# Decode attention plus a token mixer: the values of two heads as one load of 64 KB rows

## The chip, the cores and the metric

The kernel runs on one core of a Trainium2 chip. The metric is the device time of one execution in microseconds. Before the change it is 1288.31 us, the median of 3 runs (1288.29 to 1288.52). The engines are named as in the profile: PE (matrix products), PEld (its weight loads), DVE (vector), ACT (scalar), POOL, and SP, which issues the loads.

## The reference

One decode step for 8 sequences: `x + attention(norm(x)) + mixer(norm(x))`, with 32 query heads, 8 key/value heads, 8192 cached positions and heads of 128, all in float32.

```
xn = layernorm(x)
q = (xn @ wq) -> (B, Hq, 1, Dh);  k, v = the caches, each kv head serves 4 query heads
p = softmax(q k^T * Dh**-0.5);    attn = (p v) -> (B, 1, Hq*Dh) @ wo
h = layernorm(xn);  y = (gelu(h * w1 + b1)) w2 + b2      # over the token axis, F = 1792
out = x + attn + y
```

The two caches are 256 MiB each, wq and wo 8 MiB each.

## The kernel before

The work is cut into 64 items, one for each sequence and kv head; `s` is the item. Item `s` uses the buffers `k = s % 2`. An item's keys and values are 4 MB each, loaded as 128 rows of 32 KB, row `p` holding 64 cached positions. K has two buffers in SBUF and V has two; wq first lies in the V buffers, and wo at the end in the K buffers.

For one item:

- `turn` (L238, DVE): four transposes in place of a quarter of K each, 32x32 blocks.
- `qk` (L244, PE): 16 products, in 4 column groups, all of which need all four quarters; the scores go to the PSUM bank `S[k]`.
- `sm_max`, `sm_bias`, `sm_exp` (L250 to L259): maximum per partition on DVE, a product on PE that spreads it, an addition and a minimum on DVE, the exponential on ACT with its sum per partition.
- `sm_place` and `sm_turn` (L263, L267): a product with a permutation on PE, and a transpose on DVE, which bring the weights into the form in which PE can hold them.
- `pv` (L274, PE): 16 products of the weights with V, into the bank `O[k]`.
- `o_pick`, `o_place`, `o_sums`, `o_norm` (L279 to L300): the blocks of `O` that count are masked, added up and divided by the sum of the weights; the result goes to the table `OX`.
- the mixer's share of the item (`mx_begin`, `mx_steps`, `mx_end`, `y_add`), on PE, ACT, POOL and DVE.

A function `slot` issues one such item in an order that is written out by hand, with the items overlapped: in slot `s` DVE turns K of item `s` and the weights of item `s - 1`, PE makes the scores of `s` and the value products of `s - 1`, and the output of `s - 2` is normed. The loop `For_i` has four slots, each a stage. A stage may not be entered by an engine before all engines have finished the stage before the last one; `previous_stage_wait` says where in its instructions an engine reports that.

All large loads are issued by SP in program order: V of item `s` at the head of slot `s`, once the value products of `s - 2` have left that buffer, and K of item `s + 2` after the score product of `s`. Ahead of the loop stand wq, K of items 0 and 1 and V of item 0; after it the last two slots issue wo in two halves (`load_wo`, L80), the second in ever smaller pieces. The end, after the last slot, is written out: the last value products (L274), the last norms, `regroup` (L438), which gathers the outputs of 7 of the 8 sequences within the last slot and of the eighth at the end, the product with wo (L471, L481), and the store of the result (L483).

Of the kernel before, what the change touches and what calls it, by code (L numbers as in the profile page):

```python
# [30 lines left out]
PAD = 96  # L31
# [3 lines left out]
def attn_mixer_kernel(ctx: ExitStack, tc: tile.TileContext, x, kc, vc, wq, wo, w1, b1, w2, b2, out):  # L35
# [11 lines left out]
    turns = [0]  # L47

    def misc():
        turns[0] += 1  # L50
        return MI[turns[0] % 2]

# [4 lines left out]
    V = [ring.tile([P, NT, DH], F32, name=f"v{k}") for k in range(2)]  # L57
    WQ = []

    def load_wq():  # L60
        for a in range(2):
            t = V[a].rearrange("p (c n) d -> p c (n d)", c=NC // 2)
            nc.sync.dma_start(t, wq.rearrange("(p c) n -> p c n", c=NC)[:, a * NC // 2:(a + 1) * NC // 2, :])
            WQ.extend(t[:, c, :] for c in range(NC // 2))

    def load(to, src, n, pieces=(NT,)):
        rows = src.rearrange("b h (p t) d -> (b h) p t d", p=P)[n]
        at = 0
        for w in pieces:
            nc.sync.dma_start(to[:, at:at + w, :], rows[:, at:at + w, :])  # L70
            at += w

# [3 lines left out]
    def load_wo(a, pieces):  # L76
        rows = wo.rearrange("(p a c) n -> a p c n", p=P, a=2)[a]
        at = 0
        for w in pieces:
# [34 lines left out]
                          ident.rearrange("p (g i x) -> p i g x", i=NB, g=NG))  # L114
    dm = const.tile([P, NG], F32, name="dm")
# [41 lines left out]
    RD = const.tile([P, REP], F32, name="rd")  # L157
# [44 lines left out]
    def q_project(between):  # L202
# [6 lines left out]
        for a in range(2):  # L209
            q = t2k.tile([P, n], F32, name="t2k")  # L210
            nc.scalar.copy(q, S[a])
            mt = O[a]
# [5 lines left out]
            mq = misc()  # L218
# [33 lines left out]
    def sm_bias():  # L252
        m = misc()
        nc.tensor.matmul(m[:, :P], MR.to_broadcast([P, P]), nident, start=True, stop=True)  # L254
        nc.vector.tensor_tensor(SQ, m[:, :P], hmask, ALU.add)  # L255
        nc.vector.tensor_reduce(NBIAS, SQ, AX.X, ALU.min)  # L256

    def sm_exp(k):
        nc.scalar.activation(PR[k], S[k], AF.Exp, bias=NBIAS, scale=SCALE, accum_out=LR[:, k:k + 1])  # L259

    def sm_place(k):
        m = misc()
        nc.tensor.matmul(m, perm, PR[k], start=True, stop=True)  # L263
        return m

    def sm_turn(k, m):
        nc.vector.transpose(PT[k], m)  # L267

    def pv(k, u0=0, u1=NU):
        for u in range(u0, u1):
            c = u % NB
            nc.tensor.matmul(O[k][c * Q:(c + 1) * Q, :], PT[k][:, u * Q:(u + 1) * Q],  # L274
                             V[k][:, u * NG:(u + 1) * NG, :].rearrange("p t d -> p (t d)"),
                             start=(u < NB), stop=(u >= NU - NB))

    def o_pick(k):
        nc.vector.tensor_tensor(OM.rearrange("p (g d) -> p g d", g=NG), O[k].rearrange("p (g d) -> p g d", g=NG),  # L279
# [4 lines left out]
    def o_place(k):  # L284
        nc.tensor.matmul(MH[:, k * REP:(k + 1) * REP], OB[:, :DH], sel, start=True, stop=True)  # L285

    def o_last(k):
        nc.vector.tensor_copy(OM[:, :256], O[k][:, :256])
        nc.scalar.copy(OM[:, 256:], O[k][:, 256:])
# [7 lines left out]
    def o_norm(k, s):  # L297
        nc.vector.reciprocal(RD, MH[:, 64 + k * REP:64 + (k + 1) * REP])  # L298
        nc.vector.tensor_tensor(OS, MH[:, k * REP:(k + 1) * REP], RD, ALU.mult)  # L299
        nc.vector.tensor_tensor(OX[:, s], OS.unsqueeze(2).to_broadcast([P, REP, NB]),  # L300
# [211 lines left out]
```

## Time and profile before

| | |
|---|---|
| median of 3 runs | 1288.31 us |
| the profiled execution's own time | 1288.28 us |
| its span | 1286.4 us |
| mean granted clock of PE | 0.818 |
| busy PE, DVE, ACT, POOL | 67%, 70%, 26%, 17% of the span |
| moved by DMA | 553.84 MB, mean 431 GB/s |

The span runs from the first to the last instruction of the profiled execution; its own time is 1.9 us longer. Busy shares are over the whole span: a PE or DVE that is busy two thirds of the time may still be waited for in every slot. In the timeline a row is a start, a length, an engine, a line of the kernel and what it writes and reads, and in brackets how long the engine had been idle and what ended that.

### The profile page before, as it was taken

How to read it: one execution, taken by the hardware profiler on the slowest of the kernel's cores; microseconds unless marked ns; L12 is line 12 of the kernel's file. 1: busy time of each engine (PE TensorE's matmuls, PEld its weight loads, DVE VectorE, ACT ScalarE, POOL GpSimd, SP SyncE). 2: the span in 40 equal slices, each digit the busy share in tenths (PEclk: the TensorE clock that was granted, in tenths of full speed). 3: DMA queues.
4: the chain of work that ended last, by engine and by line, in shares of the span. 5: the costliest groups of instructions: out<-in, count | busy, mean ns of one | idle time of the engine just before them, and what ended most of it. 6: DMA issues, size and time to landing. Idle time of an engine off the chain costs nothing.

```text
span 1286.4 us, 15585 instructions
## 1 busy us (share of the span) xinstructions
PE 863.0 (67%) x5498; PEld 256.8 (20%) x5498; DVE 895.1 (70%) x1261; ACT 332.6 (26%) x459; POOL 218.1 (17%) x201
## 2 busy tenths in 40 slices
PE   4568667667667667667667667667567667567578
PEld 1112112212212112112112112112112112112123
DVE  3687787677686676676686776686676776676672
ACT  1142232222222222232222222231231231231221
POOL 0121221121221221221221221221211221221210
PEclk9688788788778788788788788788788788788789
DMA  9999999999999999999999999999999999999998
GB/s 409 425 438 430 433 438 426 439 427 438 431 433 439 425 439 427 438 432 432 439 425 440 426 438 433 431 439 426 439 428 436 435 429 439 426 439 430 434 434 355
DMA packets 20206, 553.84 MB, mean 431 GB/s; under 512 B 2621, under 2 KB 2653, under 8 KB 3045
## 3 DMA queue, kind: packets, MB, share of 16 engines
q1 hardware_dynamic: 19764, 553.67, 99.8%
q8 instruction: 7, 0.11, 0.0%
q10 hardware_dynamic: 400, 0.02, 0.0%
q0 software_dynamic: 32, 0.02, 0.0%
q14 instruction: 3, 0.02, 0.0%
HBM read 553.69 MB, written 0.02 MB: 430 GB/s over the span
## 4 chain that ended last, share of the span: by engine, by line
DVE 50%; PE 34%; issue 9%; DMA 7%; DVEq 0%; ACT 0%; SPq 0%; ACTq 0%
DVE k L238 39%; PE s L244 28%; DMA k<-in_A_k_cache_dram 4%; DVE mr L250 3%; DVE pt L267 3%; PE misc L254 2%; DMA k<-in_A_wo_dram 2%; PE mh L285 2%; DVE sq L255 1%; PE o L274 1%; DVE nb L256 1%; DMA small<-in_B_w_dram 1%; DVE os L299 1%; DVE ox L300 1%; PE misc L263 1%
## 5 line engine op out<-in xcount | busy, mean ns | idle before, releaser
L238 DVE STREAM_TRANSPOSE k<-k 128x2048 f32<-128x2048 f32 x256 | 574.1, 2280 | 73.8 <-issue 52.6
L244 PE MATMUL s<-k,w 128*32 128x512 f32 x2048 | 368.5, 886 | 333.0 <-DVE k L238 324.6
L274 PE MATMUL o<-v,pt 128*32 128x512 f32 x2048 | 246.0, 598 | 0.0
L331 POOL TENSOR_TENSOR macc<-g,mw 112x512 f32<-112x512 f32 x64 | 66.5, 1040 | 976.7 <-ACT g L328 976.7
L244 PEld LDWEIGHTS s<-k,w 128*32 128x32 f32 x2048 | 86.7, 155 | 607.1 <-issue 404.2
L306 DVE TENSOR_TENSOR yacc<-mh,yacc 128x128 f32<-128x128 f32 x64 | 18.6, 291 | 228.6 <-PE mh L285 228.6
L259 ACT ACTIVATE pr<-s,nb 128x512 f32<-128x512 f32 x64 | 44.0, 688 | 493.6 <-DVE rd L298 361.8
L328 ACT ACT_TABLE_LOAD x64 | 82.1, 1283 | 303.7 <-PE misc L324 294.5
L328 ACT ACTIVATE g<-misc,mw 112x512 f32<-112x512 f32 x128 | 99.5, 777 | 79.7 <-POOL macc L331 76.9
L335 POOL TENSOR_TENSOR macc<-macc,g 112x512 f32<-112x512 f32 x64 | 83.2, 1300 | 5.1
L336 ACT ACT_TABLE_LOAD x64 | 82.1, 1283 | 1.2
L274 PEld LDWEIGHTS o<-v,pt 128*32 128x32 f32 x2048 | 53.5, 109 | 133.3 <-issue 125.8
L331 POOL TENSOR_TENSOR g<-g,mw 112x512 f32<-112x512 f32 x64 | 66.6, 1040 | 56.9 <-ACT g L328 56.9
L263 PE MATMUL misc<-pr,perm 128*128 128x512 f32 x128 | 73.0, 652 | 2.9 <-ACT pr L259 2.9
L254 PE MATMUL misc<-nident,mr 128*128 128x128 f32 x128 | 31.2, 325 | 63.7 <-DVE mr L250 63.7
L324 PE MATMUL misc<-hn,bm 8*112 8x512 f32 x128 | 71.7, 640 | 0.0
L281 DVE TENSOR_TENSOR ob<-om 128x256 f32<-128x256 f32 x63 | 51.1, 810 | 2.2
L250 DVE TENSOR_REDUCE mr<-s 128x1 f32<-128x512 f32 x64 | 43.5, 680 | 6.1 <-PE s L244 6.1
L267 DVE STREAM_TRANSPOSE pt<-misc 128x512 f32<-128x512 f32 x64 | 43.2, 676 | 4.9 <-PE o L274 2.5
L255 DVE TENSOR_TENSOR sq<-misc,hmask 128x128 f32<-128x128 f32 x64 | 18.7, 291 | 37.2 <-PE misc L254 37.2
L279 DVE TENSOR_TENSOR om<-o,dm 128x512 f32<-128x512 f32 x63 | 41.1, 652 | 1.2 <-PE o L274 1.2
L282 DVE TENSOR_TENSOR ob<-ob 128x128 f32<-128x128 f32 x63 | 34.6, 549 | 2.2
(95 smaller groups left out, 367.9 us busy)
## 6 DMA issues: line engine op xcount, KB each, us to landing
v<-in_A_v_cache_dram SPq DMA_DIRECT2D x64, 4096.0 KB, 25.9
k<-in_A_k_cache_dram SPq DMA_DIRECT2D x63, 4096.0 KB, 22.8
v<-in_A_wq_dram SPq DMA_DIRECT2D x2, 4096.0 KB, 16.8
k<-in_A_k_cache_dram SPq DMA_DIRECT2D x2, 2048.0 KB, 26.0
k<-in_A_wo_dram SPq DMA_DIRECT2D x1, 4096.0 KB, 25.5
k<-in_A_wo_dram SPq DMA_DIRECT2D x1, 2048.0 KB, 19.2
k<-in_A_wo_dram SPq DMA_DIRECT2D x1, 1024.0 KB, 21.2
k<-in_A_wo_dram SPq DMA_DIRECT2D x1, 512.0 KB
```

Source lines behind the costliest of these rows:

```text
L238: nc.vector.transpose(t, t)
L244: nc.tensor.matmul(S[k][g * Q:(g + 1) * Q, :], W[k][:, j, :], kt[:, g, :, j * Q:(j + 1) * Q], start=(j == 0), stop=(j == NB - 1))
L250: nc.vector.tensor_reduce(MR, S[k], AX.X, ALU.max)
L254: nc.tensor.matmul(m[:, :P], MR.to_broadcast([P, P]), nident, start=True, stop=True)
L263: nc.tensor.matmul(m, perm, PR[k], start=True, stop=True)
L267: nc.vector.transpose(PT[k], m)
L274: nc.tensor.matmul(O[k][c * Q:(c + 1) * Q, :], PT[k][:, u * Q:(u + 1) * Q], V[k][:, u * NG:(u + 1) * NG, :].rearrange("p t d -> p (t d)"), ...
L324: nc.tensor.matmul(MI[2][:FP, :], BM[k].to_broadcast([B, FP]), hn, start=True, stop=True)
L328: nc.scalar.activation(G, MI[2][:FP, :], AF.Gelu_apprx_tanh, bias=MW[k][:, 1, j:j + 1], scale=MW[k][:, 0, j:j + 1])
L331: nc.gpsimd.tensor_tensor(G if j else ACC, G, MW[k][:, 2, j:j + 1].to_broadcast([FP, D]), ALU.mult)
L335: nc.gpsimd.tensor_add(ACC, ACC, G)
L336: nc.scalar.activation(sink, epst[:1], AF.Exp)
```

## The change

Items are now taken in pairs, an even one and the next odd one.

- The two V buffers are one tile, `VV`. `load_values(s)` loads the values of items `s` and `s + 1`, which lie behind each other in the cache, as 128 rows of 64 KB: the even item is in the first 64 partitions, the odd one in the other 64. The first pair and those of the loop come so, 31 loads; the last two items still have a load each.
- `sm_place` puts both items' weights into two banks `M[0]`, `M[1]`, each item into its half of the partitions: 4 products of 64 rows and 256 columns for an item (before: one of 128 and 512), with new constants `perms`. The exponential writes its two halves apart for that. `sm_turn` is called once for each bank.
- `pv` is one run of 32 products for the pair into one bank `O`; `o_pick`, `o_place` and `o_norm` are called once for a pair, with a new constant `sel2`.
- The loop body is two pairs, and a pair is two stages, `stage_a` and `stage_b`. The first items (`first`) and the last pair are written out; the last pair uses the former ways of placing, turning and multiplying under new names (`place1`, `turn1`, `pv1`), since its values come apart.

```diff
-    V = [ring.tile([P, NT, DH], F32, name=f"v{k}") for k in range(2)]
+    VV = ring.tile([P, 2 * NT, DH], F32, name="v")
+    V = [VV[:, k * NT:(k + 1) * NT, :] for k in range(2)]
...
+    def load_values(s):
+        nc.sync.dma_start(VV, vc.rearrange("b h (p t) d -> (b h) p t d", p=P // 2)[bass.ds(s, 2)].rearrange("x p t d -> (x p) t d"))
...
     def sm_place(k):
-        m = misc()
-        nc.tensor.matmul(m, perm, PR[k], start=True, stop=True)
-        return m
+        rows = slice(k * P // 2, (k + 1) * P // 2)
+        for h in range(2):
+            for i in range(2):
+                nc.tensor.matmul(M[h][rows, :].rearrange("p (u i c) -> p i u c", u=NU, i=2)[:, i], perms[:, k, i],
+                                 PR[k][:, h * 256:(h + 1) * 256].rearrange("p (u c) -> p u c", u=NU), start=True, stop=True)
...
+    def stage_a(s):
+        load_values(s)
+        for a in range(4):
+            turn(0, a * quart)
+        mx_end(1)
+        mx_begin(0)
+        for k in range(2):
+            o_sums(k)
+        qk(0)
+        mx_steps(0, True)
+        y_add()
+        q_place(s + 1, 1)
+        mx_pick(1, s + 1)
+        for a in range(2):
+            turn(1, a * quart)
+        sm_max(0)
+        tc.previous_stage_wait(nc.vector.engine)
+        sm_bias(True)
+        sm_exp(0)
+
+    def stage_b(s):
+        load(K[0], kc, s + 2)
+        sm_place(0)
+        for a in range(2, 4):
+            turn(1, a * quart)
+        mx_end(0)
+        mx_begin(1)
+        qk(1)
+        load(K[1], kc, s + 3)
+        o_pick()
+        o_place()
+        mx_steps(1, True)
+        q_place(s + 2, 0)
+        mx_pick(0, s + 2)
+        y_add()
+        sm_max(1)
+        sm_bias()
+        sm_exp(1)
+        o_norm(s - 2)
+        sm_place(1)
+        sm_turn(0)
+        tc.previous_stage_wait(nc.vector.engine)
+        pv(0, NB)
+        tc.previous_stage_wait(nc.tensor.engine)
+        sm_turn(1)
+        pv(NB)
...
+    for a in range(3):
+        turn(1, a * quart)
+    sm_max(0)
+    mx_end(0)
+    mx_begin(1)
+    sm_bias()
+    sm_exp(0, False)
+    turn(1, 3 * quart)
+    qk(1)
+    load_wo(1, (NW - 16, 4, 2, 1, 1))
+    o_pick()
+    o_place()
+    o_norm(N_IT - 4)
+    place1(0)
+    mx_steps(1, False)
+    sm_max(1)
+    turn1(0)
+    sm_bias()
+    sm_exp(1, False)
+    pv1(0, 0, NU // 2)
+    place1(1)
+    turn1(1)
+    pv1(0, NU // 2, NU)
+    regroup(0, B - 1, nc.scalar.copy)
```

Three places show how the instructions move. A row is a line, an operation, what it writes and reads, the shape of the output and how many follow each other. On SP, the loads of two items in the loop, first as before (`v_83`, `v_84` and `k_81`, `k_82` are the buffers of V and K):

```order
L70 DMA v_83<-in_A_v_cache_dram 128x8192
L70 ISA
L70 DMA k_81<-in_A_k_cache_dram 128x8192
L70 ISA
L70 DMA v_84<-in_A_v_cache_dram 128x8192
L70 ISA
L70 DMA k_82<-in_A_k_cache_dram 128x8192
```

and as changed:

```order
L70 DMA v<-in_A_v_cache_dram 128x16384
L66 ISA
L66 DMA k_81<-in_A_k_cache_dram 128x8192
L66 ISA
L66 DMA k_82<-in_A_k_cache_dram 128x8192
```

One load of both items' values now stands ahead of two loads of keys, where values and keys took turns. On PE, one pair in the loop as changed, from the scores of the even item (`s_185`) over the placing into `m_189` and `m_190` (L282) to the value product (L293); `mx` is the mixer's bank:

```order
L256 MATMUL s_185<-k_81,w_162 32x512 x16
L265 MATMUL misc<-nident,mr 128x128
L282 MATMUL m_189<-pr_165,perms 64x16x16 x2
L282 MATMUL m_190<-pr_165,perms 64x16x16 x2
L382 MATMUL mh<-macc,bw_181 32x128 x4
L366 MATMUL mx<-hn,bm_180 112x512
L256 MATMUL s_186<-k_82,w_163 32x512 x16
L304 MATMUL mh<-sel_125,ob 128x8
L265 MATMUL misc<-nident,mr 128x128
L282 MATMUL m_189<-pr_166,perms 64x16x16 x2
L282 MATMUL m_190<-pr_166,perms 64x16x16 x2
L293 MATMUL o<-v,pt 32x512 x32
```

Before, a slot's PE had these rows, in which the value product of the item before (L274) stands on both sides of the placing (L263):

```order
L244 MATMUL s_176<-k_82,w_152 32x512 x16
L285 MATMUL mh<-sel,ob 128x4
L254 MATMUL misc_180<-nident,mr 128x128
L274 MATMUL o_177<-v_83,pt_153 32x512 x8
L263 MATMUL misc_181<-pr_156,perm 128x512
L274 MATMUL o_177<-v_83,pt_153 32x512 x8
```

The value products of a pair have moved behind both its score products into one run of 32, and nothing of another item stands between a score product and its placing any more. On DVE, after the loop, the last item's K (`k_82`) as before:

```order
L238 STREAM_TRANSPOSE k_82<-k_82 128x2048
L267 STREAM_TRANSPOSE pt_153<-misc_181 128x512
L238 STREAM_TRANSPOSE k_82<-k_82 128x2048 x3
L279 TENSOR_TENSOR om<-o_178,dm 128x512
```

and as changed:

```order
L250 STREAM_TRANSPOSE k_82<-k_82 128x2048 x3
L262 TENSOR_REDUCE mr<-s_185 128x1
L268 TENSOR_TENSOR sq<-misc,hmask 128x128
L269 TENSOR_REDUCE nb<-sq 128x1
L250 STREAM_TRANSPOSE k_82<-k_82 128x2048
L298 TENSOR_TENSOR om<-o,dm 128x512
```

The maximum, the addition and the minimum of item 62 stand between the third and the fourth transpose of item 63's keys. On PE, the same end holds `regroup` (L489) between the value products of items 62 (`o`) and 63 (`m_190`), as changed:

```order
L323 MATMUL m_189<-pr_166,perm 128x512
L331 MATMUL o<-v,pt 32x512 x8
L489 MATMUL misc<-fold,ox 128x32 x7
L331 MATMUL m_190<-v,pt 32x512 x8
L336 MATMUL mh<-sel,ob 128x4
```

Before, it stood ahead of the last score product (L244):

```order
L324 MATMUL misc_182<-hn,bm_170 112x512
L438 MATMUL misc_180<-fold,ox 128x32 x7
L244 MATMUL s_176<-k_82,w_152 32x512 x16
```

The gathering of seven sequences' outputs has moved from ahead of the last scores to behind them.

More of the change, by code (lines that the diff above doesn't have):

```diff
@@ L266, in sm_turn, with sm_bias, sm_exp @@
-    def sm_turn(k, m):
-        nc.vector.transpose(PT[k], m)
-    def pv(k, u0=0, u1=NU):
+    def sm_bias(loop=False):
+        nc.tensor.matmul(MI[:, :P], MR.to_broadcast([P, P]), nident, start=True, stop=True)
+        if loop:
+            tc.previous_stage_wait(nc.tensor.engine)
+        nc.vector.tensor_tensor(SQ, MI[:, :P], hmask, ALU.add)
+        nc.vector.tensor_reduce(NBIAS, SQ, AX.X, ALU.min)
+    def sm_exp(k, halves=True):
+        to, of = PR[k], S[k]
+        if halves:
+            to, of = to.rearrange("p (h c) -> p c h", h=2), of.rearrange("p (c h) -> p c h", h=2)
+        nc.scalar.activation(to, of, AF.Exp, bias=NBIAS, scale=SCALE, accum_out=LR[:, k:k + 1])
@@ L356, in attn_mixer_kernel @@
     q_project(first_turns)
[L357 removed]
+    load_values(0)
     q_place(0, 0)
[L362 to L418 removed]
@@ L420, in first @@
-    def first(k, s):
-        turn(1 - k, 0)
-        sm_max(k)
+    def stage_a(s):
[4 more added lines that the diff above has]
+        mx_begin(0)
+        for k in range(2):
+            o_sums(k)
+        qk(0)
[9 more added lines that the diff above has]
+        sm_exp(0)
@@ L424, in first @@
+    def first():
+        qk(0)
+        load(K[0], kc, 2)
+        turn(1, 0)
+        sm_max(0)
         sm_bias()
-        sm_exp(k)
-        q_place(s + 1, 1 - k)
-        turn(1 - k, quart)
-        m = sm_place(k)
+        sm_exp(0)
+        q_place(1, 1)
+        turn(1, quart)
+        sm_place(0)
         mx_table()
-        mx_pick(k, s)
-        mx_begin(k)
-        mx_steps(k, False)
-        mx_pick(1 - k, s + 1)
-        return m
+        mx_pick(0, 0)
+        mx_begin(0)
+        mx_steps(0, False)
+        mx_pick(1, 1)
+        nc.vector.tensor_copy(yacc, mixed)
+        for a in range(2, 4):
+            turn(1, a * quart)
+        qk(1)
+        load(K[1], kc, 3)
+        sm_max(1)
+        sm_bias()
+        sm_exp(1)
+        q_place(2, 0)
+        sm_place(1)
+        for h in range(2):
+            sm_turn(h)
+        pv()
+        mx_end(0)
+        mx_begin(1)
+        mx_steps(1, False)
+        mx_pick(0, 2)
+        y_add()
@@ L443, in attn_mixer_kernel @@
     tc.prologue_barrier()
-    m = slot(0, 0, None, 0)
-    m = slot(1, 1, m, 1)
+    first()
     with tc.For_i(2, N_IT - 2, 4, iteration_sync="staggered") as s:
-        for n in range(4):
-            m = slot(s + n, n % 2, m, 2, loop=True)
-            if n < 3:
-                tc.stage_boundary()
-    m = slot(N_IT - 2, 0, m, 2, left=1)
-    m = slot(N_IT - 1, 1, m, 2, left=0)
-    sm_turn(1, m)
-    pv(1, 0, NU // 2)
-    o_pick(0)
-    o_place(0)
+        for n in range(2):
+            stage_a(s + 2 * n)
+            tc.stage_boundary()
+            stage_b(s + 2 * n)
+            if not n:
+                tc.stage_boundary()
@@ new lines, in attn_mixer_kernel @@
+    load(V[0], vc, N_IT - 2)
+    load(V[1], vc, N_IT - 1)
+    for a in range(4):
+        turn(0, a * quart)
+    mx_end(1)
+    mx_begin(0)
+    for k in range(2):
+        o_sums(k)
+    qk(0)
+    load_wo(0, (NT // REP,))
+    mx_steps(0, False)
+    y_add()
+    q_place(N_IT - 1, 1)
+    mx_pick(1, N_IT - 1)
+    for a in range(3):
+        turn(1, a * quart)
+    sm_max(0)
+    mx_end(0)
+    mx_begin(1)
+    sm_bias()
+    sm_exp(0, False)
+    turn(1, 3 * quart)
+    qk(1)
+    load_wo(1, (NW - 16, 4, 2, 1, 1))
```

176 lines of the change are left out of this document (73 added, 103 removed).

## The prediction

> **What bounds the kernel now.** I read the page first: its span, the row of DMA tenths, the queue that carries the bytes, the times to landing and the chain that ended last.
>
> ```profile
> span 1286.4 us, 15585 instructions
> DMA  9999999999999999999999999999999999999998
> q1 hardware_dynamic: 19764, 553.67, 99.8%
> DVE 50%; PE 34%; issue 9%; DMA 7%; DVEq 0%; ACT 0%; SPq 0%; ACTq 0%
> v<-in_A_v_cache_dram SPq DMA_DIRECT2D x64, 4096.0 KB, 25.9
> k<-in_A_k_cache_dram SPq DMA_DIRECT2D x63, 4096.0 KB, 22.8
> ```
>
> The queue of the caches is busy for 99.8% of the span, and in no slice under nine tenths but the last. The chain shows DVE and PE, yet that is only the path by which the last instruction was reached: one slot's work is nearly as long as its two loads. The time per load comes from a window of the loop (length, busy times and counts, granted clock, DMA share, GB/s):
>
> ```profile
> 400.00:700.00 300.00, 203.23 (x1270) 59.35 (x1274) 212.03 (x295) 78.55 (x108) 53.07 (x47) 0.80 1.00 433
> ```
>
> 4194304 bytes at 433 GB/s are 9.69 us, so a slot (a K and a V) takes 19.4 us and a pair 38.8. A load lands 22.8 or 25.9 us after its issue, more than two loads' time, so the queue always has a further load in it. The kernel is bound by its bytes, except where the loads end. What the change can gain is time per byte; what it can lose is an empty queue in the loop, or compute that sticks out after the last load.
>
> **Term A, fewer descriptors.** The packets by size, from the DMA view of 300 to 700 us (rows of 32 KB) and of 1276 to 1281.5 us (the last, small rows of wo); packets, MB, busy share of 16 engines:
>
> ```profile
> q1 hardware_dynamic: 5962, 173.48, 100.4%
> q1 hardware_dynamic: 513, 2.12, 93.6%
> ```
>
> Busy time is a x MB + b x packets: 400 x 16 x 1.004 = 6425.6 us for the first, 5.5 x 16 x 0.936 = 82.4 us for the second. The two give b = 8.7 ns for a packet, whatever its size. A 4 MB load is 8 rows per engine and a completion packet; two of them are 18 packets, one load of 64 KB rows is 9. So 9 packets per engine go, in 31 loads (the last two V stay apart): 279. At 8.7 ns that is 2.4 us; but the share over 100% says that neighbours overlap a little, so I take 6 ns: **-1.7 us**, between 0 (each 64 KB row cut in two by the queue) and -2.4.
> The Trainium skill, "DMA: Bandwidth & Descriptors", section "Why small descriptors are slow (HBM only)", has a fixed 3 cycles per packet and calls joining descriptors worth it only up to 256 B; with that page's 850 MHz the 279 packets would give an estimated 1.0 us, and A would be -1.0. The trace differs with 8.7 ns, and its rows decide.
>
> **Term B, does the queue stay full in the loop?** One load of both V buffers must wait for the whole value product of a pair, so I add up a pair from the landing of its first K (t = 0) with the durations of this slot (start, length, engine, line):
>
> ```profile
> 566.50 2.31 DVE L238 STREAM_TRANSPOSE k<-k 128x2048 f32<-128x2048 f32 x1 [1.37 <-issue]
> 568.74 0.67 DVE L267 STREAM_TRANSPOSE pt<-misc 128x512 f32<-128x512 f32 x1
> 569.34 6.65 DVE L238 STREAM_TRANSPOSE k<-k 128x2048 f32<-128x2048 f32 x3
> ...
> 576.04 5.87 PE L244 MATMUL s<-k,w 128*32 128x512 f32 x32 [5.73 <-DVE k L238]
> ...
> 581.84 0.39 PE L285 MATMUL mh<-sel,ob 128*128 128x4 f32 x2
> 582.26 0.29 DVE L306 TENSOR_TENSOR yacc<-mh,yacc 128x128 f32<-128x128 f32 x1 [4.22 <-PE mh L285]
> 582.47 0.68 DVE L250 TENSOR_REDUCE mr<-s 128x1 f32<-128x512 f32 x1
> 583.21 0.49 PE L254 MATMUL misc<-nident,mr 128*128 128x128 f32 x2 [0.98 <-DVE mr L250]
> 584.13 0.29 DVE L256 TENSOR_REDUCE nb<-sq 128x1 f32<-128x128 f32 x1
> 584.52 0.69 ACT L259 ACTIVATE pr<-s,nb 128x512 f32<-128x512 f32 x1 [8.53 <-DVE rd L298]
> 585.48 1.12 PE L263 MATMUL misc<-pr,perm 128*128 128x512 f32 x2
> 585.91 2.31 DVE L238 STREAM_TRANSPOSE k<-k 128x2048 f32<-128x2048 f32 x1 [0.93 <-issue]
> 586.53 1.92 PE L274 MATMUL o<-v,pt 128*32 128x512 f32 x16
> 588.60 0.33 SPq L70 DMA_DIRECT2D v<-in_A_v_cache_dram  x1
> 588.70 0.42 PE L340 MATMUL mh<-macc,bw 112*32 112x128 f32 x8
> 589.06 1.11 PE L324 MATMUL misc<-hn,bm 8*112 8x512 f32 x2
> ```
>
> Four transposes 2.31 + 6.65 = 9.0; first score product 5.9: 14.9; its maximum, bias and minimum 0.1 + 0.7 + 1.3: 17.0; two more transposes of the second K: 21.5 (the two before them ran beside the first score product). The placing of the first pair's weights begins 1.0 us after the exponential does and lies beside these transposes. It is eight instructions of 256 columns, twice the columns of L263: 2.0 us at L263's pace. Behind it stand L340's and L324's kind, 0.4 + 1.1. PE is then free at about 21.7, and the second score product ends at 27.6. From L285 to L263 are 3.6 us, so the second placing starts at 31.2 and ends at 33.2; the transposes of its halves (0.67 each) overlap the next steps. The value product of 64 instructions is four times L274's block less three handovers, 7.0: **40.3**. V is issued 0.2 later (588.60 against 586.53 + 1.92). From issue to first byte no row shows; the last copy bounds it by 2.8 us (issue 1283.62, span's end 1286.4), I take 1.0: V is ready at 41.5. The queue needs it when the second K (9.7), V (19.4) and the next two K (19.4) are through: **48.5**. K0 is reissued about 18, K1 about 28, needed by 29 and 39. DVE is free at about 34.5, before 38.8. The margin is 7 us, and B = 0.
>
> That is with PE at full clock, which these windows of the same slot do not always show:
>
> ```profile
> 576.00:579.50 3.50, 3.46 (x20) 0.83 (x24) 1.97 (x7) 0.00 (x0) 0.94 (x1) 0.50 1.04 449
> 579.60:585.00 5.40, 4.42 (x40) 1.39 (x32) 1.89 (x7) 0.48 (x1) 0.00 (x0) 0.91 1.04 449
> 49.62 2.08 PE L263 MATMUL misc<-pr,perm 128*128 128x512 f32 x2 [2.86 <-ACT pr L259]
> ```
>
> After 5.7 idle us PE starts at 0.50. L263 took 2.08 instead of 1.12 in the prologue, where PE had waited 2.9 us for the exponential. In the changed order both placings follow such a wait (about 3 and 3.6 us with one small product in it). Each at half clock costs +2.0; the first also slows L324's kind by 0.9, and the first four blocks of the value product may cost 1.7 more: 41.5 + 2.0 + 0.9 + 2.0 + 1.7 = 48.1, which is the limit itself. So B is 0 in most mixtures, and its upper bound is a stall of about 0.7 us in each of 30 pairs, +20 us. DVE's turn of the next first K sits inside the same chain.
>
> **Term C, the end.** The rows of before after the last K has landed:
>
> ```profile
> 1244.03 2.31 DVE L238 STREAM_TRANSPOSE k<-k 128x2048 f32<-128x2048 f32 x1 [0.66 <-DMA k<-in_A_k_cache_dram]
> ...
> 1248.62 2.34 PE L438 MATMUL misc<-fold,ox 128*128 128x32 f32 x14
> ...
> 1253.57 5.03 PE L244 MATMUL s<-k,w 128*32 128x512 f32 x32 [2.61 <-DVE k L238]
> ...
> 1262.23 1.12 PE L263 MATMUL misc<-pr,perm 128*128 128x512 f32 x2
> 1263.28 3.64 PE L274 MATMUL o<-v,pt 128*32 128x512 f32 x32
> ...
> 1267.39 1.92 PE L274 MATMUL o<-v,pt 128*32 128x512 f32 x16
> ...
> 1272.54 0.28 DVE L306 TENSOR_TENSOR yacc<-mh,yacc 128x128 f32<-128x128 f32 x1
> 1273.11 7.05 PE L471 MATMUL s<-k,xo 128*32 128x512 f32 x48 [0.72 <-DMA k<-in_A_wo_dram]
> 1280.22 0.42 DVE L474 COPY wide<-s 128x256 f32<-128x256 f32 x1 [7.41 <-PE s L471]
> 1281.22 0.40 PE L479 MATMUL mh<-wide,fold 128*32 128x128 f32 x8
> 1282.80 0.43 PE L481 MATMUL mh<-k,xo 128*32 128x128 f32 x8 [0.20 <-DMA k<-in_A_wo_dram]
> 1283.62 0.70 SPq L483 DMA_DIRECT2D out_dram<-yacc  x1
> ```
>
> From the last K's first transpose to L471 are 29.1 us, 0.7 of them a wait for wo: 28.4 of work beside three loads (V, V, wo: 29.1), so the compute of the end only just fits. The bytes behind the last K are the same afterwards, but the work behind it grows, because the last pair's two halves are now interleaved. In DVE's new order the maximum, bias and minimum of the first half stand between the third and the fourth transpose of the last K: its transposes end at 11.25 instead of 9.5 (+1.75). The score product then starts after an idle stretch on PE and I take 5.7 instead of 5.03 (+0.7). The norm of the pair before (three operations) and the 0.67 turn of the first half now stand ahead of the last bias (+0.4, +0.65), and half a value product ahead of the last placing (+0.2). The gathering of the outputs (L438, 2.34), which ran beside the transposes, now stands on PE between the two halves' value products (+2.3). That is 6.0 less 0.25 for the y add that has left this stretch: 34.15, so L471 starts 5.05 us later against the last K. It runs its 7.05; its loads are all there by the end, which saves about 0.35 of the waits before L481: **+4.7 us**. Bounds: the score product at 5.0 to 6.6 and L471 at 6.0 to 8.0 by its clock give 2.9 to 6.6; nothing covers it, since only the store follows.
>
> **The prologue** gets some ten small DVE operations, and its first V now waits for all of wq's products; but wq and three K loads, 16 MB or four times 9.69 us, are queued ahead of that V. Nothing.
>
> Sum against the profiled execution: 1286.4 - 1.7 + 0 + 4.7 = 1289.4 of span. That execution took 1288.28, with 1.9 outside the span, and the median of before is 1288.31; so **1291.3**.
>
> **Rivals.**
> 1. The loop's queue runs dry: half clock at both placings. For it: the 0.50 window and 2.08 of L263; against: the margin of 7 us at full clock. It decides once V is ready later than 48.5. With 0.2 to 0.7 us a pair it gives +6 to +20, 1297 to 1311. The Trainium skill, "TensorE: Matmul & The Clock Gate", section "HAM oscillation — how this bites in real kernels", says that PE-idle gaps over about 3.4 us bring the half clock back; by that rule the second placing always runs at half clock. The trace agrees as far as 0.50 after 5.7 us, and shows no wait of 3.6.
> 2. Not slower: the end stays under the loads. L471 cannot start before wo is in, 29.1 us after the last K, and the small pieces end the run as before. It decides if the new chain stays under 29.5 us, say because DVE orders its waits better than I add them, and gives A alone: 1286.6. Against it: six named rows each add to the chain.
> 3. The change does not do what it says: the 64 KB rows travel as two packets each. Then A is 0, or -0.2 for the completions, and the end stays: 1292.9. No row of before shows a packet over 32 KB.
>
> **How the numbers follow.** A measurement of this kernel can tell about 0.2%, 2.6 us, from no change: the borders are 1285.7 and 1290.9. Chances: forecast 0.50 (its own range 1288.8 to 1293.2; a little more than half of it over 1290.9), rival 1 0.20, rival 2 0.22 (mostly within 0.2%, 0.07 under 1285.7), rival 3 0.08. Slower: 0.27 + 0.20 + 0.06 = 0.53; faster 0.07; same 0.40. The range: from 1286.2, which holds most of rival 2, to 1298.5, which leaves out the larger half of rival 1.
>
> **What would show it.** A: 64 KB packets, about 4000 fewer in the queue, and 434 GB/s in the loop. B: DMA share of 1.00 between 100 and 1200 us; V issued before the second K lands. A lower share, with placings of 3.5 to 4 us, is rival 1. C: from the first transpose of the last K to the output product some 34 us, with the wo wait gone from its row; 29 us with the wait still there is rival 2. I would be wrong above all if the score and output products run at another clock at the end than I took.

## The result, and the profile after

The changed kernel takes 1301.4 us (median of 5 runs, 1297.9 to 1304.5) against 1288.31 us before: a ratio of 1.0104, 95% interval 1.0082 to 1.0125. It is 13 us slower, above my range and in the band of the first rival. Its runs differ by 6.6 us, those of before by 0.3. The profiled execution took 1301.4 us, 1299.6 of it span.

The page of the changed kernel: span, DMA share and GB/s in 40 slices, the queue of the loads, the chain that ended last, the landing of a K load.

```profile
span 1299.6 us, 15867 instructions
...
DMA  9999999999999999999999999999999999999996
GB/s 405 434 390 420 419 435 434 424 444 424 421 434 423 436 442 426 423 436 436 433 436 424 445 423 423 433 440 426 443 422 436 436 449 424 436 421 435 435 436 296
...
q1 hardware_dynamic: 15300, 553.67, 99.0%
...
DMA 51%; PE 23%; DVE 14%; issue 11%; ACT 1%; DVEq 0%; SPq 0%; POOL 0%; ACTq 0%
...
k<-in_A_k_cache_dram SPq DMA_DIRECT2D x63, 4096.0 KB, 22.7
```

4464 packets fewer move the same bytes, as term A wanted. But the queue's share fell from 99.8% to 99.0% of a longer span, and DMA now stands in the chain with 51%, where it had 7%. The row of tenths hides it: a slice is 32 us long, and a stall of one or two microseconds still leaves a 9. The GB/s row shows it better: 390, 420 and 419 near the start. Windows by stage (length, busy times and counts, granted clock, DMA share, GB/s):

```profile
20.00:100.00 80.00, 51.16 (x272) 16.91 (x272) 41.85 (x55) 18.41 (x25) 10.05 (x9) 0.70 0.97 413
100.00:400.00 300.00, 218.15 (x1366) 76.38 (x1370) 194.02 (x249) 85.06 (x109) 51.19 (x46) 0.81 1.00 427
400.00:700.00 300.00, 214.84 (x1324) 72.98 (x1318) 192.35 (x251) 85.55 (x110) 52.98 (x48) 0.81 1.00 432
700.00:1000.00 300.00, 218.72 (x1380) 75.12 (x1368) 197.28 (x249) 86.26 (x109) 52.58 (x48) 0.82 1.00 432
1000.00:1240.00 240.00, 164.13 (x1072) 58.06 (x1076) 153.47 (x199) 67.05 (x88) 41.43 (x37) 0.84 1.00 434
```

The rate is worst at the start and reaches what term A promised (434) only behind 1000 us. To put it into microseconds I add up the bytes of the trace's packets up to a time, take the difference to the kernel before at the same time, and divide by 433.8 GB/s. Positive is behind the kernel before:

| us behind before, at | 100 | 140 | 250 | 800 | 1250 us |
|---|---|---|---|---|---|
| changed kernel | 3.6 | 5.2 | 5.6 | 9.1 | 8.6 |

5.2 us are lost on the second and the third V load, 3.5 more between 250 and 800 us in small pieces, and where nothing stalls the changed kernel gains slowly. Then two more parts: the last K's first transpose begins 2.74 us after that load's bytes are through on the average of the DMA engines, before 1.53, so the slowest engine is 1.2 us further behind; and from that transpose to the output's store are 42.8 us, before 39.6. 8.7 at the last K's bytes, 1.2 and 3.2 are the 13.1.

**The start.** Timeline of the changed kernel, the first items, with the placing of item 0 (L282), the mixer's table (L362, copied in L468), the turns of item 1's keys (L250), the value product (L293) and the second V load (L70):

```profile
50.11 3.67 PE L282 MATMUL m<-pr,perms 128*64 128x256 f32 x8 [3.24 <-ACT pr L276]
...
53.72 0.65 PE L362 MATMUL mh<-yx,spread 8*32 8x128 f32 x8
...
54.44 0.29 DVE L468 COPY yacc<-mh 128x128 f32<-128x128 f32 x1 [3.21 <-PE mh L362]
54.64 4.49 DVE L250 STREAM_TRANSPOSE k<-k 128x2048 f32<-128x2048 f32 x2
...
59.19 6.47 PE L256 MATMUL s<-k,w 128*32 128x512 f32 x32 [2.85 <-DVE k L250]
...
72.66 8.30 PE L293 MATMUL o<-v,pt 128*32 128x512 f32 x64
...
81.25 0.19 DVE L356 TENSOR_TENSOR bw<-window 112x32 f32<-112x32 f32 x1 [7.74 <-PE mh L382]
...
82.06 2.31 DVE L250 STREAM_TRANSPOSE k<-k 128x2048 f32<-128x2048 f32 x1 [0.34 <-issue]
82.25 0.36 SPq L70 DMA_DIRECT2D v<-in_A_v_cache_dram  x1
```

and a window behind it:

```profile
84.00:86.00 2.00, 0.00 (x0) 0.00 (x0) 2.00 (x2) 0.85 (x2) 1.04 (x1) 0.85 0.00 0
```

DVE stands 3.21 us before the copy L468, since the table's products come behind a placing at half clock, and the turns of item 1 wait behind it. The value product ends at 81.0, and only then is the second V load issued, at 82.25. The window shows the cost: from 84 to 86 us no DMA engine moves a byte. The row of 81.25 makes the next pair late too: DVE waits 7.74 us for a mixer product that stands on PE behind the value product, so the first turn of the loop begins at 82.06 although its keys have long landed.

**A pair of the loop** with a late load, in the timeline, and a window ahead of that load:

```profile
272.70 8.89 DVE L250 STREAM_TRANSPOSE k<-k 128x2048 f32<-128x2048 f32 x4 [8.71 <-DMA k<-in_A_k_cache_dram]
...
281.73 6.13 PE L256 MATMUL s<-k,w 128*32 128x512 f32 x32 [9.59 <-DVE k L250]
...
288.75 0.49 PE L265 MATMUL misc<-nident,mr 128*128 128x128 f32 x2 [0.89 <-DVE mr L262]
...
291.28 3.67 PE L282 MATMUL m<-pr,perms 128*64 128x256 f32 x8 [2.04 <-ACT pr L276]
...
297.44 5.11 PE L256 MATMUL s<-k,w 128*32 128x512 f32 x32
...
303.95 0.46 PE L265 MATMUL misc<-nident,mr 128*128 128x128 f32 x2 [1.07 <-DVE mr L262]
...
306.50 2.94 PE L282 MATMUL m<-pr,perms 128*64 128x256 f32 x8 [2.09 <-ACT pr L276]
...
309.37 7.70 PE L293 MATMUL o<-v,pt 128*32 128x512 f32 x64
...
317.22 0.33 SPq L70 DMA_DIRECT2D v<-in_A_v_cache_dram  x1
```

```profile
315.00:317.00 2.00, 2.00 (x24) 0.57 (x20) 2.00 (x2) 0.00 (x0) 0.00 (x0) 1.00 0.83 360
```

V is issued 44.5 us behind the pair's first transpose, later than the prediction's 40.5, and that mostly by half clock: placings of 3.67 and 2.94 us, which take 1.94 at full clock, and a second score product of 5.11, which takes 3.64. The queue is running dry before that, at 360 GB/s from 315 us on. By the prediction's limit it had until 47.5.

**The end** of the changed kernel:

```profile
1253.98 6.70 DVE L250 STREAM_TRANSPOSE k<-k 128x2048 f32<-128x2048 f32 x3 [0.18 <-DMA k<-in_A_k_cache_dram]
...
1264.72 6.16 PE L256 MATMUL s<-k,w 128*32 128x512 f32 x32 [2.92 <-DVE k L250]
...
1276.06 1.92 PE L331 MATMUL o<-v,pt 128*32 128x512 f32 x16
1277.91 1.75 PE L489 MATMUL misc<-fold,ox 128*128 128x32 f32 x14
1279.59 1.92 PE L331 MATMUL m<-v,pt 128*32 128x512 f32 x16
...
1287.36 6.80 PE L562 MATMUL s<-k,xo 128*32 128x512 f32 x48 [0.37 <-DVE xo L491]
...
1296.77 0.70 SPq L574 DMA_DIRECT2D out_dram<-yacc  x1
```

33.4 us from the first transpose to the output product (34.15 predicted, 29.1 before), and its wait is now for DVE, not for wo.

### The profile page after: what moved, and what is told of

Same layout as the page of the kernel before. It is cut to its first block, busy times and chain, and to the rows that moved or that the text cites. A ratio compares the mean times of both kernels' runs of the same rounds, so it can differ in the third digit from the quotient of the medians.

```text
span 1299.6 us, 15867 instructions
## 1 busy us (share of the span) xinstructions
PE 916.6 (71%) x5808; PEld 317.3 (24%) x5808; DVE 816.9 (63%) x1085; ACT 355.7 (27%) x459; POOL 216.8 (17%) x201
## 4 chain that ended last, share of the span: by engine, by line
DMA 51%; PE 23%; DVE 14%; issue 11%; ACT 1%; DVEq 0%; SPq 0%; POOL 0%; ACTq 0%
DMA k<-in_A_k_cache_dram 50%; PE s L256 11%; DVE k L250 11%; PE m L282 5%; PE mx L366 2%; PE o L293 2%; DVE mr L262 1%; DMA small<-in_B_w_dram 1%; PE misc L265 1%; ACT pr L276 1%; PE mh L382 1%; PE s L562 1%; DVE sq L268 0%; DVE nb L269 0%; PE o L331 0%
## 5 line engine op out<-in xcount | busy, mean ns | idle before, releaser
L250 DVE STREAM_TRANSPOSE k<-k 128x2048 f32<-128x2048 f32 x256 | 572.9, 2284 | 163.1 <-DMA k<-in_A_k_cache_dram 162.8
L256 PE MATMUL s<-k,w 128*32 128x512 f32 x2048 | 318.5, 778 | 161.6 <-DVE k L250 95.2
L282 PE MATMUL m<-pr,perms 128*64 128x256 f32 x496 | 169.2, 501 | 128.0 <-ACT pr L276 128.0
L293 PE MATMUL o<-v,pt 128*32 128x512 f32 x1984 | 239.4, 637 | 0.2
L276 ACT ACTIVATE pr<-s,nb 128x512 f32<-128x512 f32 x64 | 72.7, 1136 | 282.8 <-DVE nb L269 178.5
L282 PEld LDWEIGHTS m<-pr,perms 128*64 128x64 f32 x496 | 79.6, 172 | 187.3 <-ACT pr L276 139.8
L370 ACT ACTIVATE g<-mx,mw 112x512 f32<-112x512 f32 x128 | 99.5, 777 | 81.9 <-POOL macc L373 77.1
L293 PEld LDWEIGHTS o<-v,pt 128*32 128x32 f32 x1984 | 63.2, 117 | 170.3 <-issue 168.6
L286 DVE STREAM_TRANSPOSE pt<-m 128x512 f32<-128x512 f32 x62 | 44.4, 717 | 87.5 <-PE m L282 86.7
L366 PE MATMUL mx<-hn,bm 8*112 8x512 f32 x128 | 81.3, 718 | 0.0
L265 PEld LDWEIGHTS misc<-nident,mr 128*128 128x128 f32 x128 | 19.0, 187 | 99.8 <-DVE mr L262 65.7
L382 PE MATMUL mh<-macc,bw 112*32 112x128 f32 x512 | 28.9, 302 | 6.7 <-POOL macc L377 6.7
```

The lines of the kernel that those rows point to most:

```text
L250: nc.vector.transpose(t, t)
L256: nc.tensor.matmul(S[k][g * Q:(g + 1) * Q, :], W[k][:, j, :], kt[:, g, :, j * Q:(j + 1) * Q], start=(j == 0), stop=(j == NB - 1))
L265: nc.tensor.matmul(MI[:, :P], MR.to_broadcast([P, P]), nident, start=True, stop=True)
L276: nc.scalar.activation(to, of, AF.Exp, bias=NBIAS, scale=SCALE, accum_out=LR[:, k:k + 1])
L282: nc.tensor.matmul(M[h][rows, :].rearrange("p (u i c) -> p i u c", u=NU, i=2)[:, i], perms[:, k, i], PR[k][:, h * 256:(h + 1) * 256].rearr ...
L293: nc.tensor.matmul(O[c * Q:(c + 1) * Q, :], PT[:, u * Q:(u + 1) * Q], VV[:, u * NG:(u + 1) * NG, :].rearrange("p t d -> p (t d)"), start=( ...
```

## The experiments

The theory before them: V is issued too late, in the first pairs because of the order of the first items, in the loop because of half clock; and the end is a loss of its own. The rival: the 64 KB rows themselves are slow to start.

**e1: the first items in another order.**

```diff
-        nc.vector.tensor_copy(yacc, mixed)
         for a in range(2, 4):
             turn(1, a * quart)
+        nc.vector.tensor_copy(yacc, mixed)
...
         q_place(2, 0)
-        sm_place(1)
-        for h in range(2):
-            sm_turn(h)
-        pv()
         mx_end(0)
         mx_begin(1)
         mx_steps(1, False)
         mx_pick(0, 2)
         y_add()
+        sm_place(1)
+        for h in range(2):
+            sm_turn(h)
+        pv()
```

> Theory (a late V: the queue runs dry wherever a pair's V is issued later than about 44 us behind the pair's first key transpose): in the changed kernel the first two pairs lose 2.8 and 2.9 us, because the first items' code lets the first turn of item 1 wait behind a copy of the mixer's result, and the loop's first stage behind a mixer product that stands after the first value product. Here only the order of the first items is changed: the copy stands behind the four transposes of item 1, and the mixer's steps stand ahead of the second placing. By the theory about 5.7 us go (1295 to 1297), the second and third V stand in the queue ahead of their turn, and the later pairs' stalls of about 1 us stay. Rival (64 KB rows are slow in themselves, or the first pairs stall for a cause in the queue): within 1 us of the changed kernel's 1301.

Measured: 1292.6 us (1290.7 to 1293.8), 8.8 less than the changed kernel. The windows of e1, at the place of the stall and over the next pairs:

```profile
84.00:86.00 2.00, 2.00 (x15) 0.62 (x11) 2.00 (x2) 1.44 (x2) 1.91 (x2) 0.50 1.06 459
...
100.00:400.00 300.00, 219.53 (x1358) 74.35 (x1350) 194.70 (x248) 84.33 (x109) 52.77 (x47) 0.81 1.00 432
```

459 GB/s stand where there were 0; V is issued at 78.2. The start is settled. That more went than 5.7 us was not foreseen: the later stalls are nearly gone too (0.8 us in all, up to the sixth pair). From then on V is issued 41.8, 38.4 and 39.4 us behind the first transpose, over and over.

**e2: throwaway products that keep PE's clock up.**

```diff
+    def warm(k, n):
+        rows = slice(k * P // 2, (k + 1) * P // 2)
+        for _ in range(n):
+            nc.tensor.matmul(M[1][rows, :256], perms[:, k, 0], rj.rearrange("p j i d -> p (j i d)")[:, :256], start=True, stop=True)
...
         sm_max(0)
+        warm(0, 1)
         tc.previous_stage_wait(nc.vector.engine)
         sm_bias(True)
+        warm(0, 3)
         sm_exp(0)
```

The same stands around the bias of the second item.

> Extra throwaway products are added, one ahead of and three behind the bias product of each item, between the scores and the placing; their results are overwritten by the placing. They keep PE busy in the idle stretch, so that PE's clock does not fall to half. Theory (late V because of half clock at the placings, my first rival): both placings take 1.9 us instead of 3.7 in nearly all pairs, V is issued some 38 us behind the pair's first transpose instead of 42 to 45, and the stalls of about 1 us in the loop go: 4 to 5 us less than the changed kernel, some more if the first pairs gain too (1294 to 1297). Rival (the stalls come from the transfers, not from the time of the issue): V is issued earlier, the DMA share stays where it was, and the time is within 1 us of 1301. Second rival (the extra products are themselves in the way): placings later by their 0.5 to 0.9 us each, V no earlier.

Measured: 1293.8 us (1291.9 to 1294.0). The placing's group of products, by line, in the changed kernel and, in the second block, in e2 (busy, mean ns | idle before it):

```profile
L282 PE MATMUL m<-pr,perms 128*64 128x256 f32 x496 | 169.2, 501 | 128.0 <-ACT pr L276 128.0
```

```profile
L282 PE MATMUL m<-pr,perms 128*64 128x256 f32 x496 | 123.8, 394 | 41.8 <-ACT pr L276 41.8
```

Each placing in the loop takes 1.94 us, V is issued at 37.4 to 38.9, and behind 150 us there is no stall of more than 0.1 us. The 3.0 us of the first pair stay. So it is the time of the issue, not the transfer, that made the loop's stalls: with V in time every 64 KB packet of the loop takes 2418 ns. Half clock is one thing that makes the issue late; e4 shows another.

**e3: the gathering of the outputs ahead of the last scores.**

```diff
     turn(1, 3 * quart)
+    regroup(0, B - 1, nc.scalar.copy)
     qk(1)
...
     pv1(0, NU // 2, NU)
-    regroup(0, B - 1, nc.scalar.copy)
     y_add()
```

> Only the gathering of seven sequences' outputs is moved back ahead of the last score product, where it stood before the change. Term C holds 2.3 us for it. Theory: it was 1.75 us on PE between the last two value products, so 1.5 to 2 us go from the end: from the last key's first transpose to the output product about 31.7 instead of 33.4 us, and the rest of the time as in the changed kernel. Rival (the end is set by another chain, DVE's picks and norms): less than 0.5 us.

Measured: 1298.2 us, between 1291.9 and 1308.1: the loop's stalls change so much from run to run that this time says nothing of 2 us. The profiled execution does; its end:

```profile
1273.83 5.19 PE L256 MATMUL s<-k,w 128*32 128x512 f32 x32 [0.79 <-DVE k L250]
...
1284.36 1.92 PE L331 MATMUL o<-v,pt 128*32 128x512 f32 x16
1286.10 1.90 PE L331 MATMUL m<-v,pt 128*32 128x512 f32 x16
...
1293.78 7.05 PE L562 MATMUL s<-k,xo 128*32 128x512 f32 x48 [0.30 <-DVE xo L491]
```

From one L331 to the next are 1.74 us instead of 3.53, and the score product takes 5.19 instead of 6.16, probably because the gathering, now ahead of it, keeps PE busy and its clock up. From the last K's first transpose (1263.09) to the output product are 30.7 us, to the store 40.3 instead of 42.8: 2.5 us, more than the 1.5 to 2 expected; the shorter score product accounts for the rest.

**e4: the exponential in natural order.**

```diff
-        to, of = PR[k], S[k]
-        if halves:
-            to, of = to.rearrange("p (h c) -> p c h", h=2), of.rearrange("p (c h) -> p c h", h=2)
-        nc.scalar.activation(to, of, AF.Exp, bias=NBIAS, scale=SCALE, accum_out=LR[:, k:k + 1])
+        nc.scalar.activation(PR[k], S[k], AF.Exp, bias=NBIAS, scale=SCALE, accum_out=LR[:, k:k + 1])
...
-                                 PR[k][:, h * 256:(h + 1) * 256].rearrange("p (u c) -> p u c", u=NU), start=True, stop=True)
+                                 PR[k].rearrange("p (u c h) -> p h u c", u=NU, h=2)[:, h], start=True, stop=True)
```

> Only the exponential's output is changed: it is written in natural order (the changed kernel writes two halves apart, and takes 1.14 us where before it took 0.69), and the placing's products read their columns with a stride of two instead. Theory: the exponential takes 0.69 again and the placing is no slower, so V is issued about 0.9 us earlier in each pair; with a limit of about 44 us this takes away perhaps half of the loop's stalls of 1 us: 1 to 4 us less than the changed kernel. Rival (the strided read slows the products by as much): no change in V's issue or in the time.

Measured: 1293.9 us (1291.9 to 1295.7). The exponential's group in the changed kernel and in e4:

```profile
L276 ACT ACTIVATE pr<-s,nb 128x512 f32<-128x512 f32 x64 | 72.7, 1136 | 282.8 <-DVE nb L269 178.5
```

```profile
L273 ACT ACTIVATE pr<-s,nb 128x512 f32<-128x512 f32 x64 | 44.0, 687 | 328.1 <-DVE nb L269 185.5 <-PE misc L265 142.6
```

0.45 us less for each item, and the products that read with a stride take hardly longer (2.02 us for a placing at full clock instead of 1.94). The gain, 7.5 us, is larger than expected: V is issued at 41 us at the latest, and the loop does not stall behind 250 us. My prediction had kept 0.69 us for a write in two halves, which costs 1.14.

**e5: e1, e2 and e3 together; e6: the same with 32 KB rows.** For e6 the two halves of the V tile lie 8 floats apart, so that a row of the load can't be longer than 32 KB; of its edits the one of the tile is shown, the others fit the views of it and shorten a filler tile:

```diff
-    VV = ring.tile([P, 2 * NT, DH], F32, name="v")
+    VV = ring.tile([P, 2, NT * DH + 8], F32, name="v")
```

> The changes of the first three experiments together: the first items in the new order, the throwaway products that keep PE's clock up (overwritten by the placing), and the gathering of the outputs ahead of the last scores. Theory (three separate losses, each with its own cure): no stall of the V loads anywhere, so the bytes arrive 1.4 us earlier than in the kernel before (which is what the run with the new first items gained on it between 250 and 1250 us), the last engine's lag costs 0.2, and the end is 0.8 to 1.0 longer than before instead of 3.2: 1287.5 to 1288.2, that is the kernel before or 0.1% under it. Rival (the causes overlap, or the end has another chain): 1289 or more.

> The kernel of e5_best with 8 unused floats between the two halves of the V tile, so that the one load of a pair is made of 256 rows of 32 KB instead of 128 of 64 KB. Waits, order and work are the same; only the size of the rows differs. This isolates term A. By the cumulated bytes of the runs so far the 64 KB rows are worth 1.4 us: 1.4 us above e5_best. By my two windows' 8.7 ns for each of 248 to 279 packets: 2.4 at most, by the 6 ns that I took 1.7. The Trainium skill, 'DMA: Bandwidth & Descriptors', section 'Why small descriptors are slow (HBM only)', gives an estimated 1.0. If the gain comes from joining two loads and not from the rows, the two kernels are equal.

Measured: e5 1287.7 us (11 runs, 1286.9 to 1289.6; ratio to before 1.0001, 0.9992 to 1.0010), as expected: the three cures together give back the whole 13 us. Its trace is of a run of 1287.0 us; what the five runs over 1289 lose is not shown. e6 1292.6 us (1292.2 to 1294.0): 4.9 above e5, and not by any of the prices named above. Its 32 KB packets took 1216 ns in the mean, many of them 1216 to 1224; in all other kernels they took 1213 where nothing stalled. So e6 had changed a second thing, the place of data in SBUF, and didn't isolate term A.

**e7 and e8: V later on purpose.** Added to e5, 20 or 32 value products ahead of those of a pair, which overwrite them:

```diff
+    def again(n):
+        for i in range(n):
+            u, c = i % NU, i % NB
+            nc.tensor.matmul(O[c * Q:(c + 1) * Q, :], PT[:, u * Q:(u + 1) * Q],
+                             VV[:, u * NG:(u + 1) * NG, :].rearrange("p t d -> p (t d)"), start=True, stop=True)
...
+        again(20)
         pv(0, NB)
```

> The kernel of e5_best with 20 more throwaway value products ahead of those of each pair in the loop (overwritten by them), 0.22 us each: the V load is issued 4.4 us later, at 41.8 to 43.4 us behind the pair's first key transpose instead of 37.4 to 38.9. By the limit of my prediction (issue at 47.5 at the latest) and by the one that the changed kernel's stalls showed (about 44) alike there is no stall: within 1.5 us of e5_best. If the stalls grow evenly with the time of the issue, each pair loses some tenths and the time is 1295 or more.

> The same with 32 throwaway value products, 7.1 us: V is issued at 44.4 to 46.0 us behind the first transpose. Here the two limits part. Prediction's limit (V needed when the second K, V and the next two K are through, issue at 47.5): no stall, within 2 us of e5_best. Limit of about 44, because the DMA engines do not run in step and the first of them is through 2 us or more ahead of the last: each of 30 pairs loses 0.4 to 2 us, 1300 to 1345, with periods of 39.1 to 40.7 us from V load to V load instead of 38.68.

Measured: e7 1288.0 us, e8 1305.1 us. Windows over 900 us of the loop, e7 and then e8:

```profile
300.00:1200.00 900.00, 763.57 (x5379) 296.53 (x5371) 590.00 (x739) 252.31 (x323) 155.53 (x138) 0.94 1.00 434
```

```profile
300.00:1200.00 900.00, 799.91 (x5839) 309.68 (x5838) 576.70 (x736) 252.14 (x322) 154.45 (x138) 0.96 1.00 428
```

In e7 V is issued 41.6 to 43.2 us behind the first transpose, and no pair stalls: 4.4 us of added work on PE cost nothing. In e8 it is issued at 44.1 to 46.2, 1.3 to 3.4 us ahead of the prediction's limit, and 25 of 28 pairs are longer than 38.68 us, 39.2 in the mean. The limit is about 44, and as e8's PE runs at 0.96 of its clock, a late V stalls the queue whatever makes it late.

**e9: the halves 64 floats apart instead of 8.**

> As e6_best_32k, with 64 unused floats between the halves of the V tile instead of 8 (256 bytes instead of 32). In e6_best_32k the 32 KB packets took 1216 to 1224 ns about as often as 1213, which none of the other kernels shows, and its V loads cost 0.15 us a pair more than two loads in the kernel before. Theory (the 32-byte offset of the second half slowed those packets; the 64 KB row itself saves only 8 ns against two of 32 KB, 2418 against 2 x 1213): all packets take 1213 again, the pair's period is 38.75 instead of 38.83 and the time is 1.5 to 2.5 us above e5_best, 1289 to 1290. Rival (256 rows of 32 KB as one load are slower than as two loads, whatever their offset): 1292 to 1293 again.

Measured: 1289.0 us (11 runs, 1288.4 to 1292.1), and every 32 KB packet takes 1213 ns again. One early stall of 1.5 us stands in its profiled execution; behind that the table of bytes shows the rates alone:

| us behind before, at | 100 | 250 | 1250 us | gained in 1000 us |
|---|---|---|---|---|
| e5, 64 KB rows | 0.0 | -0.1 | -1.3 | 1.2 |
| e9, 32 KB rows, one load | 1.6 | 1.6 | 1.3 | 0.2 |
| e6, 32 KB rows 8 floats apart | 0.4 | 0.8 | 3.4 | -2.6 |

1.2 us in 1000 are 0.046 a pair and 1.4 us in 31 loads. Of these the rows make about 1.1 and the joined load the rest; the fastest runs of e5 and e9 (1286.9 and 1288.4) are 1.4 apart. Between e6 and e9 the 32 bytes are worth 0.11 us a pair, which is 3.3 ns for each of the pair's 32 packets per engine: 1216.3 in the mean instead of 1213.0. Which loads are slowed is not separated: only 31% of e6's packets kept 1213 ns though half of them are K's, and e6 and e9 also shorten a filler tile among the constants by 8 and 64 floats, so K may have moved as well.

**e10: another order at the end; e11: this end without throwaway products, with e4's exponential.**

```diff
-    for a in range(3):
+    for a in range(2):
         turn(1, a * quart)
     sm_max(0)
+    for a in range(2, 4):
+        turn(1, a * quart)
     mx_end(0)
     mx_begin(1)
+    regroup(0, B - 1, nc.scalar.copy)
     sm_bias()
     sm_exp(0, False)
-    turn(1, 3 * quart)
-    regroup(0, B - 1, nc.scalar.copy)
     qk(1)
...
-    o_norm(N_IT - 4)
     place1(0)
...
     sm_exp(1, False)
+    o_norm(N_IT - 4)
```

> e5_best with another order at the end: the maximum of item 62 stands between the second and third transpose of the last keys, so that the fourth ends 1.0 us earlier; its addition and minimum stand behind the fourth; the norm of the pair before stands behind the last exponential (0.55 us off the last maximum's way). Theory (the chain of the end, which nothing covers, is what term C counts): 1.0 + 0.5 us less from the last key's first transpose to the output product, 30.1 instead of 31.6, and 1286.0 to 1286.6 in all, 0.1% under the kernel before. Rival (PE's clock at the end decides: score product 5.2 to 6.2, output product 5.4 to 7.0): within 0.5 us of e5_best.

> e10_end without the throwaway products, but with the exponential written in natural order as in e4_expn. Theory (the placings run at half clock again, but with the first pairs mended and 0.9 us less in each chain the V load is issued by 41 us, under the limit of 44): no stall in the loop, as many bytes at each time as in e10_end, and a time within 0.7 us of it, with runs that agree to 1 us. Rival (only the throwaway products keep the loop from stalling): some pairs stall, 1289 or more, and the runs scatter by more than 2 us as in e1_pro.

Measured: e10 1287.2 us (11 runs, 1286.9 to 1289.2), e11 1287.1 us (11 runs, ten of them 1286.9 to 1287.3; ratio to before 0.9992, 0.9983 to 1.0001). e10 misses its 1286.0 to 1286.6, though the output product does start 29.8 us behind the last K's first transpose, 1.8 earlier than in e5. Its rival held, PE's clock at the end. The output product of e5 and a window inside it, then the same of e10:

```profile
1274.26 5.36 PE L571 MATMUL s<-k,xo 128*32 128x512 f32 x48 [0.31 <-DVE xo L500]
...
1274.30:1276.00 1.70, 1.70 (x16) 0.51 (x20) 0.08 (x1) 0.00 (x0) 0.00 (x0) 1.00 0.93 395
```

```profile
1272.63 7.05 PE L572 MATMUL s<-k,xo 128*32 128x512 f32 x48 [0.31 <-DVE xo L500]
...
1274.30:1276.00 1.70, 1.70 (x12) 0.43 (x8) 0.00 (x0) 0.00 (x0) 0.00 (x0) 0.50 0.92 386
```

In e10 it takes 1.7 us longer: the granted clock of the window is 0.50 instead of 1.00, and both products end at nearly the same time (1279.6 and 1279.7). wo, which held the end of the kernel before, is close behind it. The window of 1280 to 1282 us, in the kernel before and in e11:

```profile
1280.00:1282.00 2.00, 2.00 (x68) 1.52 (x60) 0.42 (x1) 0.37 (x1) 0.00 (x0) 1.00 0.73 285
```

```profile
1280.00:1282.00 2.00, 2.00 (x76) 1.83 (x68) 0.35 (x1) 0.37 (x1) 0.00 (x0) 1.00 0.24 91
```

The bytes of e11 are nearly through where those of before are not: the last packet of wo ends at 1281.1 instead of 1282.5, and the store follows 1.3 and 1.1 us later. So a faster output product could gain some 0.2 us more, an estimate from these two distances, and then the bytes decide. e11 shows that no throwaway products are needed: V at 37.3 to 39.7, no stall in the loop. It is the fastest kernel of the study, though 0.08% is within what these runs can tell apart.

## Why the prediction was wrong, point by point

- **Term A** was right in mechanism and nearly in size: -1.7 predicted, -1.4 measured. A 64 KB row travels as one packet (rival 3 is out): 2418 ns, two of 32 KB 2426. By these times a row saves 8 ns, and a completion takes 9, so my 8.7 ns fits a packet's own time. But packets overlap, as the share over 100% said, and what the bytes gained is 1.4 us / 279 = 5 ns for each; the step down to 6 ns was right in kind and a little short. The estimated 1.0 us from the Trainium skill, "DMA: Bandwidth & Descriptors", section "Why small descriptors are slow (HBM only)", is 0.4 us off where mine is 0.3.
- **Term B**, put at 0, is the first of two steps that failed. It is: "The queue needs it when the second K (9.7), V (19.4) and the next two K (19.4) are through: 48.5". That sum counts from the first transpose as if all DMA engines were at the same byte then. But a transpose waits for the last engine, and the first one is ahead: in e5 the next V's first packet starts 46.2 us behind the transpose with no stall, and the sixteenth, by its order that of the last of the 16 engines, at 48.0. From issue to first packet of a dry queue are 0.96 us, as I had taken (1.0). So the first engine goes idle if V is issued later than about 45, and the pairs of the changed kernel stall from 44.3 on, where stalls have spread the engines further. In e7 no pair stalls up to 43.2; in e8, issued from 44.1 on, most pairs are longer, and the earliest issue with an idle engine is at 44.3 too. The chain up to the issue was 2 to 3 us shorter than I had added: 37.7 instead of 40.5 at full clock, where the second score product takes 3.64 and I had 5.9, and 45.0 instead of 47.1 at the worst mixture. So the margin was there by my own numbers, and it was the limit that took it away. Rival 1 is what happened in the loop, with its place (both placings); the point from which it decides was 3.5 us too late, and that had kept its chance at 0.20. Its price was not met: the loop's stalls behind 250 us cost 3.5 and the last engine's lag 1.2, less than its +6. That the time fell into its band of 1297 to 1311 was luck, since the prologue's loss lies in it too.
- **The prologue**: "Nothing" was the second wrong step, and with 5.2 of the 13 us the largest single loss. I had looked at its first V, which was on time, and not at the second, which waits for a value product behind the chain of items 0 and 1 at half clock. e1 shows that the order of those few lines was the cause.
- **Term C** was of the right kind and too large: 4.7 predicted, 3.2 measured. The gathering was sized at 2.3 and cost 1.8 on PE, the output product ran 6.80 instead of 7.05, L562 came 0.8 sooner than I summed, and the steps behind it, which no longer wait for wo, saved 0.85 instead of 0.35. e3 shows that the gathering, with what it does to PE's clock, made 2.5 of the 3.2.
- **Rival 2** (the end hidden, A alone: 1286.6) is nearly reached in its number by e10 and e11 once the losses are mended, 1287.2 and 1287.1, but not by its mechanism: their output products wait for DVE, not for wo.
- Not in my sum at all: the 1.2 us by which the last DMA engine fell further behind the others after the stalls.

On the clock: in the pair shown above, the first placing runs at a granted clock of 0.50 throughout, behind waits of 0.89 and 2.04 us with one small product between them. The second, behind 1.07 and 2.09, begins at 1.00 and falls to 0.50 after 0.8 us. In e11, with a chain shorter by two times 0.45 us, the second placing takes 2.02 us (full clock) in every pair, as does the first in two of three. The Trainium skill, "TensorE: Matmul & The Clock Gate", section "HAM oscillation — how this bites in real kernels", names PE-idle gaps over about 3.4 us, by which I wrote that the second placing would always run at half clock. The runs bear out neither the rule nor my use of it: half clock came with no wait over 2.1 us since the score product, and not in every pair.

## What to carry to other kernels

When two transfers become one, its buffer is free only when the last reader of both halves is done: compare the time of that issue with the moment at which the first DMA engine runs out of work, and not with the landing of a load, which the slowest engine sets (here 1.8 us apart in e5, up to 2.7 in the changed kernel). Do the sum for the first rounds too, where the order is another one. And do it at the slow clock: a margin of 7 us at full clock was 0 at half.

## What the runs showed of the hardware that was not expected

- A queue that has run dry costs more than the gap. In the loop of the changed kernel the first packets of a late V load took up to 3.66 us instead of 2.42; from 250 to 850 us such longer packets make about 3 us of each engine's time, and time without a packet about 1 more than in e5. The DMA engines then stayed out of step: the lag of the last one at the last K was 1.4 to 1.8 us in the kernel before, e5, e7, e10 and e11, 2.7 in the changed kernel, 3.2 in e3.
- With a gap of 32 bytes between the two halves of a load's destination, the loop's 32 KB packets were 3.3 ns slower in the mean (e6); with 256 bytes they were not (e9).
- An exponential that writes with a stride of two halves takes 1.14 us instead of 0.69 (e4), while the eight products that read with a stride of two take 2.02 instead of 1.94.
- In e1 the loop settles into a pattern of three pairs. The granted clock changes in the trace at multiples of 3.41 us, and three pairs (3 x 38.68 = 116.04) are 34 of these: once a phase without a stall is met, it comes again, and each stall moves the phase on. That would explain why the changed kernel stops stalling behind 850 us and why its runs differ by 6.6 us; it was not tried by itself.
